# State-space scan and GELU feed-forward on one core: w_out loaded with four neighbouring rows to a partition, w_in cast with stepped writes, the last chunk stored from ScalarE

## The chip, the cores and the metric

The kernel runs on one core of a Trainium2 chip. The metric is the device time of one execution in microseconds (us); lower is better. Engines: PE is TensorE (PEld its weight loads), DVE is VectorE, ACT is ScalarE, POOL is GpSimd, SP is SyncE, which here only issues transfers. SPq and ACTq are the instructions with which SP and ACT issue transfers. A core has 16 DMA engines, which all queues share.

## The reference, cut to what matters

The first half is a chunked linear recurrence over four sequences of 768 tokens and 8 heads; its output, arranged as 3072 tokens by 256 features, goes into a feed-forward layer. Only the second half meets the change:

```python
n_tokens, d_model, d_ff = (3072, 256, 2048)
h = x @ w_in                       # (3072, 256) @ (256, 2048)
g = 0.5 * h * (1.0 + np.tanh(c * (h + 0.044715 * h * h * h)))
return (g @ w_out).astype(np.float32)   # (3072, 2048) @ (2048, 256)
```

The sum over the 2048 hidden features in the last product may be taken in any order, as long as column f of w_in meets row f of w_out.

## The kernel before, in words

The 3072 tokens are 24 chunks of 128 (`gc`, 0 to 23), taken in 12 pairs (`u`, 0 to 11). For each pair, the scan makes a masked gram matrix (`f_G` on PE, `f_M` on DVE), the outputs (`f_Y`), and a carried state (`f_S`, `f_SP`); its result is evicted as bf16 into `xm` with the features on the partitions (`f_yev`, L592). The feed-forward of the same pair follows: `f_s1` (L630) multiplies 128-column blocks of `w_in_sb` with the 256 tokens of the pair, two blocks to a PSUM bank; `f_gelu` (L645) evicts each bank through the GELU into `gT`, hidden features on the partitions; `f_s2` (L652) multiplies 16 blocks of `gT` with 16 slices of `w_out_sb` and sums them for one chunk; `f_oev` (L672) evicts the sum to `o_sb`, and `f_store` (L680) writes it out.

The weights come as float32 and are cast to bf16. Both are loaded in four quarters of 512 KB. `load_wi` (L208) brings 512 columns of w_in (rows of 2 KB) and is issued by ACT; `load_wo` (L280, the transfer at L283) brings 512 rows of w_out and is issued by SP. `wo` (L278) lays row `k*128 + f` on partition `f`, so each partition gets four separate rows of 1 KB. `f_wi` (L293) and `f_wo` (L296) cast a quarter each through `copy` (L285; POOL at L289, DVE at L291). POOL casts all quarters, but for the last of w_out, which it shares with DVE (`WENG`, L702).

The kernel writes its instructions in an order that a planner chooses at build time (`run_order`, L34): every step is a `Node` with an engine, a guessed duration, what it depends on and a priority, and each engine then executes its instructions in that fixed order. Loads are nodes as well: `LO` (L699) is the planner's guess, in us, for one quarter of w_out; `LI` that for w_in. `HEAD` (L700) is the order of the first loads: x 0, x 1, b 1, the three later quarters of w_in, b 2, w_out 0, w_out 1, c 2, w_out 2, w_out 3, x 2. Those in `SEND` go by ACT's queue, the rest by SP's. A load is issued only when the one eight before it has landed (`LANES`). The load of b 2 is also held by `f_gate` (L164), a one-element memset on POOL behind the first cast of w_in (L993, `GS = 0`), and the loads after it on SP stand behind it in the queue.

Chunks below `NPS` = 19 are stored by POOL, later ones by SP. The last chunk (L971 to L976) is evicted in two halves of 128 columns, one by ACT and one by DVE (`f_oevs`, L661), and each half is stored by a transfer of its own (`f_half`, L667), from ACT and from SP. Between planned gaps PE executes dummy products with zeros (`fill`, L1009) that keep it busy in the first 20 us of the plan.

Of the kernel before, what the change touches and what calls it, by code (L numbers as in the profile page):

```python
# [8 lines left out]
FP32 = mybir.dt.float32  # L9
# [104 lines left out]
def kernel(  # L114
# [10 lines left out]
    nc = tc.nc  # L125
# [3 lines left out]
    Q = 128  # L129
    CPB = S // Q  # L130
    NCH = batch * CPB
    T3 = CPB // 2
    W = S // T3
# [20 lines left out]
    opool = ctx.enter_context(tc.tile_pool(name="opool", bufs=6))  # L154
# [50 lines left out]
    WF = {}  # L205
# [58 lines left out]
    w_in_sb = const.tile([128, 2, d_ff], BF16, name="w_in_sb")  # L264
# [7 lines left out]

    X16 = {}
    state = {}
    gts, ops, hps, halves = {}, {}, {}, {}


    wo = moe_w_out.rearrange("(k f) m -> f k m", f=128)  # L278

    def load_wo(q, e):  # L280
        if ("o", q) not in WF:
            WF[("o", q)] = wfp.tile([128, 4, d_model], FP32, name="wf")
        e.dma_start(out=WF[("o", q)], in_=wo[:, 4 * q:4 * q + 4])  # L283

    def copy(eng, o, i):  # L285
        if eng == "ACT":
            nc.scalar.activation(o, i, AF.Copy)  # L287
        elif eng == "POOL":
            nc.gpsimd.tensor_copy(out=o, in_=i)  # L289
        else:  # L290
            nc.vector.tensor_copy(out=o, in_=i)  # L291

    def f_wi(q, k0, k1, eng):  # L293
        copy(eng, w_in_sb[:, k0:k1, q * 512:(q + 1) * 512], WF[("i", q)][:, k0:k1])

    def f_wo(q, k0, k1, eng):  # L296
        copy(eng, w_out_sb[:, 4 * q + 2 * k0:4 * q + 2 * k1], WF[("o", q)][:, 2 * k0:2 * k1])
# [360 lines left out]
                             rhs=w_out_sb[:, fi, :], start=(fi == 0), stop=(fi == NF - 1),  # L658
                             skip_group_check=True)

    def f_oevs(gc, h, eng):  # L661
        hs = slice(h * 128, h * 128 + 128)
        o_sb = opool.tile([128, 128], FP32, name="o_half")
        copy(eng, o_sb, ops[gc][:, hs])
        halves[h] = o_sb

    def f_half(gc, h, q):  # L667
        u, r = divmod(gc, 2)
        hs = slice(h * 128, h * 128 + 128)
        q.dma_start(out=out[u * W + r * Q:u * W + (r + 1) * Q, hs], in_=halves[h])  # L670

    def f_oev(gc, eng):  # L672
        o_sb = opool.tile([128, d_model], FP32, name="o_sb")
        if eng == "ACT":
# [19 lines left out]
    DW = 1.0  # L694
    LANES = 8
    FIRST = [("c", 3), ("b", 3), ("c", 4), ("x", 3), ("b", 4), ("x", 4)]
    NPS = 19
    PET = {0: "ACT", 1: "ACT", 2: "ACT", 3: "ACT"}
    LB, LX, LI, LO, XD, XL = 0.92, 1.25, 1.42, 1.5, 0.6, 3.6  # L699
    HEAD = [("x", 0), ("x", 1), ("b", 1), ("wi", 1), ("wi", 2), ("wi", 3), ("b", 2), ("wo", 0), ("wo", 1), ("c", 2), ("wo", 2), ("wo", 3), ("x", 2)]  # L700
    SEND = {("b", 1): -185, ("wi", 1): -184.9, ("wi", 2): -179.5, ("wi", 3): -179.4}
    WENG = [("POOL", "POOL", "POOL", "POOL"), ("POOL", "POOL", "POOL", "POOL+DVE")]  # L702
# [1 line left out]
    TAIL = 4  # L704
# [3 lines left out]
    GS = 0  # L708
# [15 lines left out]
    def add(eng, dur, fn, *args, deps=(), prio=0.0, alloc=(), done=0.0):  # L724
        n = Node(eng, dur, (lambda: fn(*args, *[BK[j] for p, j in zip(n.alloc, n.bank)
                                               if p == "bk"])), deps, prio, alloc, done)
        nodes.append(n)
        return n
# [5 lines left out]
    def frees(n, *by, i=0):  # L734
        if n.alloc:
            n.frees[i] += list(by)
# [12 lines left out]
    win_l, won_l, wi_n, wo_n = {}, {}, {}, {}  # L749
    bl, xl, xcn = {}, {}, {}  # L750
    later = []
    Gn, Mn, Yn, yevn, Sn, SPn, Fn, bnn, gcn, Dns = ({} for _ in range(10))
# [77 lines left out]
    for j in range(NP):  # L830
# [58 lines left out]
        u = j  # L889
# [63 lines left out]
    for g, (c0, n) in enumerate(GROUPS):  # L953
        per = 512 // (n * Q)
        ends_ = []
        for tt in range(n):
            gc = c0 + tt
            if g < TWO and tt:
                prev = ahead
            ahead = list(prev)  # L960
            for q in range(4):
                need = [geln[(g, i)] for i in range(4 * n) if i * per <= 4 * q + 3]
                nd = add("PE", 0.437, f_s2, g, tt, q, deps=need[-1:] + wo_n[q] + prev,
                         prio=PB + 10 * c0 + 10 * n + 2.5 * ((tt + 2 * q) if g < TWO else 4 * tt + q) + 1.2,
                         alloc="bk" if q == 0 else ())
                if q == 0:
                    first = nd
                prev = [nd]
            ends_.append(nd)
            oeng = "DVE" if gc >= NCH - TAIL and gc % 2 else "ACT"  # L970
            if gc == NCH - 1:  # L971
                ev2 = [add(e, 0.25, f_oevs, gc, h, e, deps=[nd], prio=-40 + h) for h, e in enumerate(("ACT", "DVE"))]
                frees(first, *ev2)
                s0 = add("ACT", 0.1, f_half, gc, 0, nc.scalar, deps=[ev2[0]], prio=-39)
                add("OUT", 0.05, f_half, gc, 1, nc.sync, deps=[ev2[1], s0], prio=gc)
                continue  # L976
            else:
                oevn[gc] = add(oeng, 0.4, f_oev, gc, oeng, deps=[nd], prio=-40)
            frees(first, oevn[gc])
            if g < TWO:  # L980
                prev = list(ends_)
            if gc < NPS:
                st_n = add("POOL", 1.1, f_store, gc, nc.gpsimd, deps=[oevn[gc]], prio=2000)
            else:
                add("OUT", 0.05, f_store, gc, nc.sync, deps=[oevn[gc]], prio=gc)

    if D1 is not None:
        Dns[1].deps.append(gpn[(0, D1)])
# [1 line left out]
        n.deps.append(gpn[(u, 0)])  # L990

    held = HEAD[max(n for n, e in enumerate(HEAD) if e in SEND) + 1]
    issue[held].deps.append(add("POOL", 0.1, f_gate, *held, deps=[SPn[0] if GS else wi_n[0][-1]], prio=-98))  # L993
    for g in range(GT_BUFS, len(GROUPS)):
        c0, n = GROUPS[g - GT_BUFS]
        gpn[(g, 0)].deps.append(oevn[c0 + n - 1])
# [54 lines left out]
```

## Time and profile before

| | |
|---|---|
| median of 2 runs | 115.31 us (115.06 to 115.55) |
| the profiled execution's own time | 115.72 us |
| its span in the trace | 114.0 us |
| PE busy | 106.8 us (94%) |
| ACT, DVE, POOL busy | 73.1, 59.0, 32.2 us |
| moved by DMA | 15.01 MB in 68,736 packets |
| granted clock of PE | 1.00 throughout |

In a row of a timeline stand the start and the length in us, the engine, the line, the operation, what it writes and reads, and how many instructions are merged; in brackets stands how long the engine was idle before, and what ended the wait. A row of windows has a stretch, its length, the busy time and the number of instructions of PE, PEld, DVE, ACT and POOL, the granted clock, the mean busy share of the 16 DMA engines (transfers that overlap in one engine can bring it over 1) and GB/s. A queue row has the packets, the MB, and the time of its packets as a share of 16 engines' span.

### The profile page before, as it was taken

What the parts mean: (1) busy time and instruction counts of PE and PEld (TensorE: products, weight loads), DVE (VectorE), ACT (ScalarE), POOL (GpSimd) and SP (SyncE); (2) the same over time, 40 slices, a digit from 0 to 9 for tenths busy, and PEclk for the clock granted to TensorE, in tenths of its full rate; (3) what the DMA queues carried; (4) which work ended last, traced back from release to release, by engine and by line L of the source; (5) the groups of instructions that cost most, each with busy time, mean ns of one, the idle gap of its engine ahead of it and who ended that gap; (6) DMA issues with size and microseconds to landing.
All of it is one profiled execution on the core that took longest, in us unless ns stands there. A gap on an engine that the chain in (4) does not pass through costs nothing.

```text
span 114.0 us, 3606 instructions
## 1 busy us (share of the span) xinstructions
PE 106.8 (94%) x1497; PEld 86.5 (76%) x1497; DVE 59.0 (52%) x134; ACT 73.1 (64%) x161; POOL 32.2 (28%) x60
## 2 busy tenths in 40 slices
PE   5968998979999999999999999999999999999990
PEld 2544566958688788887887887888878878878870
DVE  2799764287796193750962944906918318000101
ACT  0557796951559368596685794774966866857720
POOL 6851636657510412103241311312211011000000
PEclk9999999999999999999999999999999999999999
DMA  3999976959977959599898877776121111011021
GB/s 69 264 311 384 354 200 207 286 98 231 181 137 146 121 109 154 82 161 117 138 125 162 131 85 152 107 102 129 46 46 46 52 45 50 6 46 46 0 92 46
DMA packets 68736, 15.01 MB, mean 132 GB/s; under 512 B 64176, under 2 KB 67088, under 8 KB 68720
## 3 DMA queue, kind: packets, MB, share of 16 engines
q1 hardware_dynamic: 63456, 9.74, 49.5%
q10 hardware_dynamic: 4352, 2.56, 7.2%
q0 software_dynamic: 912, 2.49, 5.9%
q8 instruction: 11, 0.18, 0.6%
q14 instruction: 5, 0.04, 0.1%
HBM read 10.58 MB, written 3.15 MB: 120 GB/s over the span
## 4 chain that ended last, share of the span: by engine, by line
PE 76%; DMA 11%; SPq 5%; POOL 3%; issue 2%; ACTq 1%; DVE 0%; ACT 0%; POOLq 0%
PE bk L657 37%; PE bk L640 31%; DMA wf<-in_moe_w_out_dram 7%; DMA wf<-in_moe_w_in_dram 5%; SPq L283 3%; PE bk L524 2%; POOL w_out_sb L289 2%; PE gb L454 2%; SPq L183 1%; PE bk L498 1%; ACTq L183 1%; POOL w_in_sb L289 1%; PE bk L547 1%; PE gb L465 1%; PE bk L510 0%
## 5 line engine op out<-in xcount | busy, mean ns | idle before, releaser
L648 ACT ACTIVATE gT<-bk 128x512 bf16<-128x512 f32 x96 | 50.4, 603 | 9.1 <-PE bk L640 8.9
L657 PE MATMUL bk<-w_out_sb,gT 128*128 128x256 bf16 x384 | 49.1, 273 | 0.6 <-POOL w_out_sb L289 0.6
L640 PE MATMUL bk<-xm,w_in_sb 128*128 128x256 bf16 x384 | 47.5, 273 | 0.8 <-POOL w_in_sb L289 0.8
L640 PEld LDWEIGHTS <-w_in_sb 128*128 128x128 bf16 x384 | 37.0, 98 | 6.1 <-POOL w_in_sb L289 1.5
L657 PEld LDWEIGHTS <-gT 128*128 128x128 bf16 x384 | 36.5, 98 | 6.7 <-issue 2.4
L683 POOL DMA_DIRECT2D out_dram<-o_sb x19 | 10.5, 553 | 45.4 <-ACT o_sb L675 45.4
L475 DVE TENSOR_TENSOR m<-gb,trk 128x1024 bf16<-128x1024 f32 x14 | 17.0, 1217 | 0.0
L675 ACT ACTIVATE o_sb<-bk 128x256 f32<-128x256 f32 x22 | 8.5, 386 | 11.3 <-PE bk L657 5.2
L607 DVE SCALAR_TENSOR_TENSOR s_new<-s_new,pend,bk 128x64 f32<-128x64 f32 x16 | 4.4, 276 | 20.4 <-ACT xm L287 19.7
L287 ACT ACTIVATE xm<-bk 128x256 bf16<-128x256 f32 x22 | 7.4, 381 | 9.2 <-PE bk L498 6.9
L384 DVE TENSOR_TENSOR bc<-bc,fac 128x256 bf16<-128x256 f32 x24 | 10.9, 481 | 3.0 <-DMA bc<-in_C_dram 2.0
L289 POOL CAST x<-x_t 128x512 bf16<-128x512 f32 x12 | 8.3, 690 | 10.6 <-DMA x_t<-in_x_dram 10.6
L475 DVE TENSOR_TENSOR m<-gb,tri 128x1024 bf16<-128x1024 f32 x8 | 9.7, 1219 | 1.5 <-PE gb L465 1.5
L623 DVE SCALAR_TENSOR_TENSOR sp_new<-s_new,pend,pm 128x128 bf16<-128x128 f32 x19 | 7.4, 420 | 0.1
L1013 PE MATMUL gb<-wz 128*128 128x512 bf16 (+2 forms) x17 | 5.4, 444 | 1.3 <-DVE warm L221 1.3
L430 DVE TENSOR_SCALAR ce<-bt,par 128x256 bf16<-128x256 bf16 x22 | 5.3, 284 | 2.2 <-ACT bt L287 2.2
L677 DVE COPY o_sb<-bk 128x256 f32<-128x256 f32 x1 | 0.4, 425 | 10.9 <-PE bk L657 10.9
L1013 PEld LDWEIGHTS <-wz 128*128 128x128 bf16 x25 | 2.7, 120 | 3.8 <-issue 1.9
L289 POOL CAST w_in_sb<-wf 128x1024 bf16<-128x1024 f32 x4 | 4.2, 1040 | 3.3 <-DMA wf<-in_moe_w_in_dram 3.3
L605 DVE COPY s_new<-bk 128x64 f32<-128x64 f32 x3 | 0.7, 222 | 8.1 <-ACT xm L287 8.1
L289 POOL CAST w_out_sb<-wf 128x1024 bf16<-128x1024 f32 (+1 forms) x4 | 4.0, 995 | 3.1 <-DMA wf<-in_moe_w_out_dram 3.1
L287 ACT ACTIVATE bt<-bk 128x256 bf16<-128x256 bf16 (+1 forms) x5 | 2.4, 473 | 1.7 <-PE bk L406 1.7
(81 smaller groups left out, 58.2 us busy)
## 6 DMA issues: line engine op xcount, KB each, us to landing
out_dram<-o_sb POOLq DMA_DIRECT2D x19, 128.0 KB, 2.9
wf<-in_moe_w_in_dram ACTq DMA_DIRECT2D x4, 512.0 KB, 8.3
wf<-in_moe_w_out_dram SPq DMA_DIRECT2D x4, 512.0 KB, 8.3
x_t<-in_x_dram SPq DMA_DIRECT2D x14, 128.0 KB, 3.0
x_t<-in_x_dram SPq DMA_DIRECT2D x5, 256.0 KB, 4.5
bc<-in_C_dram SPq DMA_DIRECT2D x14, 64.0 KB, 3.5
bc<-in_B_dram SPq DMA_DIRECT2D x14, 64.0 KB, 3.4
bc<-in_C_dram SPq DMA_DIRECT2D x4, 128.0 KB, 4.6
```

The costliest lines, as they stand in the source:

```text
L287: nc.scalar.activation(o, i, AF.Copy)
L289: nc.gpsimd.tensor_copy(out=o, in_=i)
L384: nc.vector.tensor_tensor(out=d["bc16"][:, i], in0=d["bc"][:, i].rearrange("p h (r n) -> p r h n", r=2) if j < TOK else d["bc"][:, i].rear ...
L430: nc.vector.tensor_scalar(out=d["ce"][:, e], in0=v, scalar1=par[:, e:e + 1], scalar2=None, op0=ALU.mult)
L475: nc.vector.tensor_tensor(out=state[("m", u, f)].rearrange("p g r e t -> p g (r e t)"), in0=state.pop(("gc", u, f), gram[f]).rearrange("p ...
L623: nc.vector.scalar_tensor_tensor(out=sp_new.rearrange("p (j d) -> p j d", j=2), in0=state[("s", gc)].rearrange("p (o d) -> p o d", o=1).to ...
L640: nc.tensor.matmul(out=hp[:, j * nt:(j + 1) * nt], lhsT=w_in_sb[:, kc, fi * 128:(fi + 1) * 128], rhs=xm[:, kc, c0 * Q:c0 * Q + nt], start= ...
L648: nc.scalar.activation(gts[g][:, i * per:(i + 1) * per, 0:nt], hps.pop((g, i)).rearrange("p (j t) -> p j t", j=per), AF.Gelu_apprx_tanh)
L657: nc.tensor.matmul(out=ops[gc], lhsT=gts[g][:, fi, tt * Q:(tt + 1) * Q], rhs=w_out_sb[:, fi, :], start=(fi == 0), stop=(fi == NF - 1), ski ...
L675: nc.scalar.activation(o_sb, ops.pop(gc), AF.Copy)
L683: q.dma_start(out=o.rearrange("(p r) m -> r p m", r=2)[r] if u < TOK else o[r * Q:(r + 1) * Q], in_=ops.pop(gc))
L1013: nc.tensor.matmul(out=bank[:, 0:128 * w], lhsT=wz[:, 0:128], rhs=wz[:, 0:128 * w], start=True, stop=True)
```

## The change

`wo` now takes the 2048 rows as four quarters of 128 groups of four: partition `f` of quarter `q` gets rows `512q + 4f` to `512q + 4f + 3`, which are 4 KB in a row in memory. Slice `4q + k` of `w_out_sb` then holds rows `512q + 4f + k`, so the columns of w_in have to be put in the same order: `f_wi` reads its quarter in a row and writes neighbouring elements 128 elements (256 bytes) apart, so that block `4q + k` of `w_in_sb` holds columns `512q + 4f + k`. The casts of w_out and all products keep their shapes.

Chunk 18 is stored by SP in place of POOL (`NPS` 18). The last chunk is evicted whole by ACT and stored by one transfer that ACT issues; `f_oevs` and `f_half` go. The planner's guess for a quarter of w_out goes from 1.5 to 1.3 us. The list at `f_gate` gets more entries, of which `GS = 0` still picks the first, the same as before.

```diff
-    wo = moe_w_out.rearrange("(k f) m -> f k m", f=128)
+    wo = moe_w_out.rearrange("(q f k) m -> q f k m", q=4, k=4)
...
-        e.dma_start(out=WF[("o", q)], in_=wo[:, 4 * q:4 * q + 4])
+        e.dma_start(out=WF[("o", q)], in_=wo[q])
...
     def f_wi(q, k0, k1, eng):
-        copy(eng, w_in_sb[:, k0:k1, q * 512:(q + 1) * 512], WF[("i", q)][:, k0:k1])
+        copy(eng, w_in_sb[:, k0:k1, q * 512:(q + 1) * 512].rearrange("d c (k f) -> d c f k", k=4),
+             WF[("i", q)][:, k0:k1].rearrange("d c (f k) -> d c f k", k=4))
...
-    def f_oevs(gc, h, eng):
...
-    def f_half(gc, h, q):
...
-    NPS = 19
+    NPS = 18
...
-    LB, LX, LI, LO, XD, XL = 0.92, 1.25, 1.42, 1.5, 0.6, 3.6
+    LB, LX, LI, LO, XD, XL = 0.92, 1.25, 1.42, 1.3, 0.6, 3.6
...
-            oeng = "DVE" if gc >= NCH - TAIL and gc % 2 else "ACT"
-            if gc == NCH - 1:
-                ev2 = [add(e, 0.25, f_oevs, gc, h, e, deps=[nd], prio=-40 + h) for h, e in enumerate(("ACT", "DVE"))]
-                frees(first, *ev2)
-                s0 = add("ACT", 0.1, f_half, gc, 0, nc.scalar, deps=[ev2[0]], prio=-39)
-                add("OUT", 0.05, f_half, gc, 1, nc.sync, deps=[ev2[1], s0], prio=gc)
-                continue
-            else:
-                oevn[gc] = add(oeng, 0.4, f_oev, gc, oeng, deps=[nd], prio=-40)
+            oeng = "DVE" if gc >= NCH - TAIL and gc % 2 and gc < NCH - 1 else "ACT"
+            oevn[gc] = add(oeng, 0.4, f_oev, gc, oeng, deps=[nd], prio=-40)
             frees(first, oevn[gc])
...
-                add("OUT", 0.05, f_store, gc, nc.sync, deps=[oevn[gc]], prio=gc)
+                last = gc == NCH - 1
+                add("ACT" if last else "OUT", 0.05, f_store, gc, nc.scalar if last else nc.sync, deps=[oevn[gc]], prio=gc)
...
-    issue[held].deps.append(add("POOL", 0.1, f_gate, *held, deps=[SPn[0] if GS else wi_n[0][-1]], prio=-98))
+    issue[held].deps.append(add("POOL", 0.1, f_gate, *held, deps=[(wi_n[0][-1], SPn[0], xcn[1], SPn[1])[GS]], prio=-98))
```

More of the change, by code (lines that the diff above doesn't have):

```diff
@@ L274 @@
     state = {}
-    gts, ops, hps, halves = {}, {}, {}, {}
-    wo = moe_w_out.rearrange("(k f) m -> f k m", f=128)
+    gts, ops, hps = {}, {}, {}
+    wo = moe_w_out.rearrange("(q f k) m -> q f k m", q=4, k=4)
     def load_wo(q, e):
@@ L659, in f_s2 @@
                              skip_group_check=True)
-    def f_oevs(gc, h, eng):
[L662 to L665, printed above, removed]
-    def f_half(gc, h, q):
-        u, r = divmod(gc, 2)
-        hs = slice(h * 128, h * 128 + 128)
-        q.dma_start(out=out[u * W + r * Q:u * W + (r + 1) * Q, hs], in_=halves[h])
     def f_oev(gc, eng):
```

## The prediction

> **What bounds the kernel now.** I read the page first: the engines, the chain that ended last, then PE in time.
>
> ```profile
> span 114.0 us, 3606 instructions
> PE 106.8 (94%) x1497; PEld 86.5 (76%) x1497; DVE 59.0 (52%) x134; ACT 73.1 (64%) x161; POOL 32.2 (28%) x60
> ...
> PE 76%; DMA 11%; SPq 5%; POOL 3%; issue 2%; ACTq 1%; DVE 0%; ACT 0%; POOLq 0%
> ```
>
> PE is busy for 94% of the span, and 76% of the chain is PE. So no edit away from PE can be worth more than the time in which PE waits. A window says where that is not:
>
> ```profile
> 50.00:110.00 60.00, 60.00 (x791) 51.37 (x790) 25.16 (x53) 41.62 (x90) 10.45 (x17) 1.00 0.46 82
> ```
>
> From 50 to 110 us PE is busy for all of 60.00 us at granted clock 1.00, and its timeline has no idle note between 24.80 us and that window either. What the change can gain lies before 24.80 us or behind the last product. PE's timeline of the start:
>
> ```profile
> 14.79 1.05 PE L640 MATMUL bk<-xm,w_in_sb 128*128 128x256 bf16 x8 [0.28 <-POOL w_in_sb L289]
> 15.67 0.33 PE L1013 MATMUL bk<-wz 128*128 128x256 bf16 x2
> 15.93 0.25 PE L535 MATMUL bk<-bt,sp_new 64*32 64x128 bf16 x8
> ...
> 17.75 2.36 PE L640 MATMUL bk<-xm,w_in_sb 128*128 128x256 bf16 x20 [0.49 <-POOL w_in_sb L289]
> ...
> 23.76 0.42 PE L465 MATMUL gb<-ce,bt 32*64 32x256 bf16 x16
> 24.80 2.78 PE L657 MATMUL bk<-w_out_sb,gT 128*128 128x256 bf16 x24 [0.62 <-POOL w_out_sb L289]
> ```
>
> Three waits in a row: 0.28 us for the third cast of w_in, 0.49 us for the fourth, and 0.62 us for the last cast of w_out. Between 17.75 and 24.18 us PE is dense, and at 24.18 it stands: its order has nothing else until the last quarter of w_out is there. So PE resumes at the later of two times: the end of its own work, now 24.18, and the last cast of w_out, now 24.80.
>
> POOL, which makes these casts (the x casts are here for their lengths):
>
> ```profile
> 7.35 1.04 POOL L289 CAST w_in_sb<-wf 128x1024 bf16<-128x1024 f32 x1 [0.43 <-DMA wf<-in_moe_w_in_dram]
> ...
> 12.36 1.04 POOL L289 CAST w_in_sb<-wf 128x1024 bf16<-128x1024 f32 x1 [0.64 <-DMA wf<-in_moe_w_in_dram]
> 13.70 1.04 POOL L289 CAST w_in_sb<-wf 128x1024 bf16<-128x1024 f32 x1 [0.29 <-DMA wf<-in_moe_w_in_dram]
> 16.66 1.04 POOL L289 CAST w_in_sb<-wf 128x1024 bf16<-128x1024 f32 x1 [1.93 <-DMA wf<-in_moe_w_in_dram]
> 18.34 1.04 POOL L289 CAST w_out_sb<-wf 128x1024 bf16<-128x1024 f32 x1 [0.65 <-DMA wf<-in_moe_w_out_dram]
> 19.69 1.04 POOL L289 CAST w_out_sb<-wf 128x1024 bf16<-128x1024 f32 x1 [0.31 <-DMA wf<-in_moe_w_out_dram]
> 21.62 1.04 POOL L289 CAST w_out_sb<-wf 128x1024 bf16<-128x1024 f32 x1 [0.89 <-DMA wf<-in_moe_w_out_dram]
> 23.88 0.87 POOL L289 CAST w_out_sb<-wf 128x512 bf16<-128x512 f32 x1 [1.23 <-DMA wf<-in_moe_w_out_dram]
> ...
> 30.70 0.62 POOL L289 CAST x<-x_t 128x512 bf16<-128x512 f32 x1
> ...
> 39.13 0.62 POOL L289 CAST x<-x_t 128x512 bf16<-128x512 f32 x1
> ```
>
> Each cast of a weight begins when its transfer lands; POOL was idle before every one. The landings of w_out, not POOL, set 24.80. And these landings are slowed by one lagging DMA engine:
>
> ```profile
> 16.50:17.00 0.50, 0.50 (x8) 0.43 (x6) 0.01 (x1) 0.38 (x2) 0.34 (x1) 1.00 0.07 23
> 17.00:17.50 0.50, 0.26 (x3) 0.09 (x1) 0.50 (x1) 0.28 (x3) 0.50 (x1) 1.00 0.07 25
> ```
>
> A DMA share of 0.07 is about one engine of 16 (0.0625), although two quarters of w_out have not landed yet: 15 engines have finished and a transfer counts as landed when the last one has. SP stands meanwhile in an issue:
>
> ```profile
> 8.86 1.61 SPq L283 DMA_DIRECT2D wf<-in_moe_w_out_dram  x1
> 10.52 2.14 SPq L283 DMA_DIRECT2D wf<-in_moe_w_out_dram  x1
> 12.70 1.32 SPq L183 DMA_DIRECT2D bc<-in_C_dram  x1
> 14.06 2.98 SPq L283 DMA_DIRECT2D wf<-in_moe_w_out_dram  x1
> ```
>
> **The change: w_out with rows of 4 KB.** A quarter goes from 512 packets of 1 KB to 128 of 4 KB, so from 32 to 8 on each engine. The price of a packet comes from the queue rows:
>
> ```profile
> q1 hardware_dynamic: 63456, 9.74, 49.5%
> q10 hardware_dynamic: 4352, 2.56, 7.2%
> q0 software_dynamic: 912, 2.49, 5.9%
> ```
>
> The shares times 16 x 114 us are 903, 131 and 108 us. With a ns for each packet and b us for each MB, q1 and q0 give a = 8.0 and b = 40.3; q10 then comes out at 35 + 103 = 138 us against 131, so the split holds to 5%. A quarter has 24 packets fewer on an engine: 24 x 8.0 = 0.19 us, and four quarters 0.77 us at the lagging engine, where they are served one behind the other (the casts at 18.34 and 19.69 stand 1.35 us apart, 32 packets by 42 ns). The last quarter then lands near 23.1 us, its cast ends near 24.0, and PE resumes at 24.18: a gain of 0.62 us, not 0.77. The lower end is 0, if the lagging engine is paced by bytes or by something else. There is more at the upper end (the issue of 2.98 us is waiting for room in the queue, by its length against the 1.32 beside it, so later loads move up too), but 24.18 caps it: none of it counts.
>
> The Trainium skill ("DMA: Bandwidth & Descriptors", section "Why small descriptors are slow (HBM only)") puts the cost of a packet in the DMA engine at about 3 cycles; at the 850 MHz which that page gives for the fabric that is an estimate of 3.5 ns, not 8.0. By it the sum would gain only some 0.34 us here in place of 0.62, and the time would be 0.3 us longer; the queue rows of this trace bear out the larger price.
>
> What is late next once this wait is gone: 24.18 itself, so the casts of w_in. After that nothing, as far as rows show; the scan's later steps on DVE are fed by PE and move along with it.
>
> **w_in cast with stepped writes.** Four instructions, same elements, each written 256 bytes from the last. No row of this trace has a POOL instruction that writes single elements in steps, so I bound the extra time x of one cast. The nearest rows are the x casts: the one at 30.70 (pair 4) reads in jumps after every 32 elements, that at 39.13 (pair 5) reads in a row, and both take 0.62 us. From 512 to 1024 elements the cast grows by 0.42 us, so 0.82 ns for an element and 0.2 us fixed. If POOL spends its time on elements, x = 0; that is also the lower end, since nothing gets shorter. The upper end I set at three times the time for an element, x = 1.7 us. I take 0, by the x casts, which are the nearest rows, though they show jumps between runs and not single elements; this is the weakest step.
>
> Where x lands: the first cast (7.35) also releases the memset that holds the load of b 2 on SP; b 2, w_out 0 and 1 and the rest of SP's queue stand behind it. An x of some 0.5 there is covered, as the lagging engine, not the issue, sets when these land. The delay of the second and third cast reaches PE at 14.79; 0.27 us of dummy products, then 0.49 us of waiting before 17.75 cover up to some 0.76. The fourth starts on its landing at 16.66, and PE behind it at 17.75 moves by all of x. PE's own work then ends at 24.18 + x, against a w_out cast at 24.0: x up to 0.62 eats the gain, more is a loss.
>
> **The last chunk and the stores.** The end of the kernel, PE first and then ACT, DVE and SP:
>
> ```profile
> 106.80 4.09 PE L657 MATMUL bk<-w_out_sb,gT 128*128 128x256 bf16 x36
> ...
> 109.23 0.38 ACT L675 ACTIVATE o_sb<-bk 128x256 f32<-128x256 f32 x1 [1.58 <-issue]
> 110.93 0.28 ACT L287 ACTIVATE o_half<-bk 128x128 f32<-128x128 f32 x1 [1.31 <-PE bk L657]
> 111.24 0.29 DVE L291 COPY o_half<-bk 128x128 f32<-128x128 f32 x1 [3.38 <-ACT o_half L287]
> 111.56 0.33 SPq L670 DMA_DIRECT2D out_dram<-o_half  x1
> ```
>
> ```profile
> out_dram<-o_sb SPq DMA_DIRECT2D x4, 128.0 KB, 1.7
> ...
> out_dram<-o_half SPq DMA_DIRECT2D x1, 64.0 KB, 1.6
> ```
>
> The halves don't run side by side: DVE's starts when ACT's has ended, so the last issue comes at 111.56. Afterwards one eviction of 0.38 us, then the issue by ACT near 110.93 + 0.38 + 0.03 = 111.34: 0.22 us earlier. The transfer is twice as large and lands in 1.7 and not 1.6 us, so the gain is 0.1 us (from 0 to 0.2). Nothing is queued behind it on ACT. Chunk 18 goes from POOL to SP: one of POOL's 19 issues (553 ns) is saved, one of about 0.33 us comes on SP. I cost it at nothing, as SP issues nothing between 84.27 and 100.29 us, and what stands behind are stores of later chunks only; without that cover it would cost its 0.33 us:
>
> ```profile
> L683 POOL DMA_DIRECT2D out_dram<-o_sb x19 | 10.5, 553 | 45.4 <-ACT o_sb L675 45.4
> ```
>
> ```profile
> 83.05 1.22 SPq L395 DMA_TRANSPOSE bt<-bc  x1
> 100.29 9.69 SPq L683 DMA_DIRECT2D out_dram<-o_sb  x4
> ```
>
> **The planner's 1.3.** The four landings are planned up to 0.8 us earlier, so PE's order may put products with w_out ahead of one or two groups of four w_in products (0.44 us each). If the real landings are earlier by 0.77 us, this costs nothing; if they are not, PE waits up to 0.44 us longer. I take 0.
>
> The sum on the profiled execution: 115.72 - 0.62 - 0.10 + 0 = 115.0 us. The median of the runs shown, 115.31, is 0.41 us below that execution, so 114.6 us.
>
> **The rivals.** (1) Stepped writes cost about half as much again for an element. Then x = 0.4 to 0.6, PE's own work ends near 24.75 and the gain is spent: about 115.1 us. Against it speaks that jumps in the x casts cost nothing; for it, that those jumps come every 32 elements. In a sentence of its own: the Trainium skill ("SBUF — State Buffer", section "Door 1: The DMA port swizzle (why `[64,N]` ≈ `[32,N]`)") says that accesses run at full rate only with at least two hits in the same line of 16 bytes, which a step of 256 bytes never has. No run so far shows whether that holds for POOL's writes.
>
> (2) The transfers don't come earlier: the lagging engine is paced by its bytes, or lags by as much again. PE's wait of 0.62 us stays, and only the end gains: 115.2 us. For it: the landings of the third and fourth quarter stand 1.93 and 2.26 us behind the one before, more than the 1.35 us for 32 packets. Against it: the packet price from the queue rows.
>
> (3) The other side: stepped writes cost more than twice as much. POOL then makes three casts of w_in back to back from 12.36: they end at 12.36 + 3 x (1.04 + x) + 0.1, past the fourth landing's 17.70 + x once x is over 1.05. With x = 1.3 (casts of 2.34 us) PE starts at 19.5 in place of 17.75, ends its own work near 25.9, and the time is 115.31 + 1.1 - 0.1 = 116.3. It decides from x = 0.72, where the sum is zero; over 2% it takes x near 1.7.
>
> **How the numbers follow.** The forecast has 0.45, rival 1 has 0.28, rival 2 has 0.15, rival 3 has 0.12. The range reaches over rivals 1 and 2 and into 3: from 114.1 (the forecast with 0.2 at the end and the spread of the runs, 0.25 to either side) to 116.1. The likeliest case's own range is 114.2 to 115.0. A measurement of this kernel can tell about 2%, or 2.3 us, from no change. Faster by that needs 1.4 us and more than all the waits that the change reaches: 0.02. Slower needs the upper end of rival 3: 0.07. Within: 0.91.
>
> **What would show each step.** In the profile of the changed kernel: 61,920 packets in q1 (63,456 less 1,536), and the issues of w_out short; casts of w_in at 1.04 us (rival 1: 1.4 to 1.6, rival 3: over 2); the last cast of w_out ending near 24.0 us and no idle note ahead of the products with its quarter; PE's last product some 0.6 us earlier; the last issue on ACT 0.41 us behind PE's end. It would be wrong if a new wait of PE shows behind 24 us, or if the casts are longer.

## The result, and the profile after

The changed kernel takes 130.31 us (130.31 to 130.32, 2 runs) against 115.31 before: a ratio of 1.1325 (95% interval 1.1272 to 1.1379), 15.0 us slower. The prediction said 114.6 us, 114.1 to 116.1. The profiled execution took 130.31 us with a span of 128.6, the one before 115.72 and 114.0: 14.6 us to account for. Here and below a median is of all runs, while a ratio leaves out the runs that fell in a slower state of the chip.

The page of the changed kernel, for the rows that the prediction showed of before: span, engines, chain, queues, and the group of the casts. In a group's row stand the busy time and the mean length in ns, then the idle time ahead of them.

```profile
span 128.6 us, 3602 instructions
...
PE 109.5 (85%) x1496; PEld 87.8 (68%) x1497; DVE 73.7 (57%) x133; ACT 73.6 (57%) x161; POOL 45.6 (35%) x59
...
PEclk9995586557999999999999999999999999999999
...
q1 hardware_dynamic: 61920, 9.80, 46.8%
...
PE 81%; DVE 13%; issue 4%; ACT 0%; ACTq 0%; DVEq 0%
...
L289 POOL CAST w_in_sb<-wf 128x1024 bf16<-128x1024 f32 x4 | 19.0, 4947 | 0.7 <-DMA wf<-in_moe_w_in_dram 0.7
```

Read it against the prediction's rows. POOL is busy 13.4 us longer; four instructions alone add 14.8, casts of 4.95 us in place of 1.04. DVE is busy 14.7 us longer with one instruction fewer, and has entered the chain with 13%, although the change gives DVE no new work and takes the eviction of a half from it. The transfers are what was meant: 61,920 packets. The clock row lies between 5 and 8 tenths from the fourth to the tenth slice.

POOL's timeline of the changed kernel:

```profile
7.29 4.73 POOL L289 CAST w_in_sb<-wf 128x1024 bf16<-128x1024 f32 x1 [0.49 <-DMA wf<-in_moe_w_in_dram]
...
12.75 14.24 POOL L289 CAST w_in_sb<-wf 128x1024 bf16<-128x1024 f32 x3 [0.22 <-DMA wf<-in_moe_w_in_dram]
26.58 3.84 POOL L289 CAST w_out_sb<-wf 128x1024 bf16<-128x1024 f32 x4
```

Three casts now run back to back and the last ends at 12.75 + 14.24 = 26.99, where it ended at 16.66 + 1.04 = 17.70. The casts of w_out find their data there and run in 3.84 us.

DVE's timeline of the same time, and behind it the row of the first of these steps in the kernel before:

```profile
7.44 5.17 DVE L359 CAST pm<-par 128x128 bf16<-128x128 f32 x1
...
13.46 1.23 DVE L476 TENSOR_TENSOR m<-gb,tri 128x1024 bf16<-128x1024 f32 x1 [0.35 <-PE gb L466]
14.60 3.03 DVE L476 TENSOR_TENSOR m<-gs,tri 128x1024 bf16<-128x1024 bf16 x1
17.55 4.85 DVE L431 TENSOR_SCALAR ce<-bt,par 128x256 bf16<-128x256 bf16 x2
22.32 4.32 DVE L385 TENSOR_TENSOR bc<-bc,fac 128x256 bf16<-128x256 f32 x1
26.57 0.41 DVE L291 CAST xm<-bk 128x256 bf16<-128x256 f32 x1
```

```profile
6.89 0.23 DVE L358 CAST pm<-par 128x128 bf16<-128x128 f32 x1
```

The cast of `pm` takes 5.17 us where it took 0.23; the two instructions for `ce` take 4.85 in place of 0.47, `bc` 4.32 in place of 0.41. They end at 12.61, 17.63 (`m` from `gs`), 22.40 and 26.64, and those are about the times at which one POOL cast ends and the next begins (the third begins at 17.30, the fourth at 21.85 and ends at 26.99). What is not held reads a PSUM bank: `m<-gb,tri` keeps its 1.23 us and the cast of `xm` from a bank its 0.41. A copy from a bank, `bt`, that starts at 11.39, before `pm` has ended, also takes 1.22 us in place of 0.28; it ends together with `pm`, at 12.61.

PE's timeline of the changed kernel:

```profile
18.09 0.39 PE L997 MATMUL gb<-wz 128*128 128x512 bf16 x1
26.70 0.39 PE L407 MATMUL bk<-ident,bc 128*128 128x128 bf16 x2 [8.21 <-DVE bc L385]
...
27.37 1.04 PE L641 MATMUL bk<-xm,w_in_sb 128*128 128x256 bf16 x4
28.33 0.65 PE L466 MATMUL gb<-ce,bt 32*64 32x256 bf16 x16
28.92 3.08 PE L641 MATMUL bk<-xm,w_in_sb 128*128 128x256 bf16 x20
...
33.25 2.35 PE L641 MATMUL bk<-xm,w_in_sb 128*128 128x256 bf16 x20
```

PE stands for 8.21 us, and not for POOL: it waits for DVE's `bc`. Only at 27.37 does it begin the products that it began at 11.96 before, and the 20 products behind the fourth cast, at 17.75 before, begin at 33.25: 15.5 us later. Behind that it runs as before. It gets 0.9 us back by its end (125.47 against 110.89, so 14.6), 0.62 of it the wait at 24.80, which isn't there as w_out was cast long ago.

One window of each kernel, before first, says what the stage lost (PE, PEld, DVE, ACT, POOL):

```profile
7.00:27.00 20.00, 17.40 (x283) 12.84 (x282) 14.02 (x29) 14.70 (x35) 10.95 (x14) 1.00 0.91 255
```

```profile
7.00:27.00 20.00, 5.31 (x87) 2.55 (x88) 19.54 (x14) 3.63 (x12) 19.49 (x7) 0.66 0.99 270
...
28.00:30.00 2.00, 2.00 (x24) 0.97 (x23) 1.13 (x2) 1.51 (x2) 2.00 (x3) 0.50 0.86 80
```

In the same 20 us PE does 87 matmuls in place of 283, DVE 14 instructions in place of 29 while it counts as busy for 19.54 us. Busy is not work here. When PE resumes, it does so at granted clock 0.50: four products take 1.04 us, where the same four took 0.61 before.

The end of the changed kernel, ACT and its queue:

```profile
125.56 0.38 ACT L665 ACTIVATE o_sb<-bk 128x256 f32<-128x256 f32 x1 [1.36 <-PE bk L658]
125.97 0.37 ACTq L673 DMA_DIRECT2D out_dram<-o_sb  x1
```

The store is issued 0.41 us behind the start of the eviction, as in the prediction's sum (0.38 + 0.03; behind PE's end it is 0.50, where the prediction's list of signs has 0.41 and its own figures make 0.45), and the span ends 3.0 us behind that start (128.6 - 125.56), against 3.1 before (114.0 - 110.93).

### The profile page after: what moved, and what is told of

Read it like the earlier page. It is cut to its first block, busy times and chain, and to the rows that moved or that the text cites. A ratio compares the mean times of both kernels' runs of the same rounds, so it can differ in the third digit from the quotient of the medians.

```text
span 128.6 us, 3602 instructions
## 1 busy us (share of the span) xinstructions
PE 109.5 (85%) x1496; PEld 87.8 (68%) x1497; DVE 73.7 (57%) x133; ACT 73.6 (57%) x161; POOL 45.6 (35%) x59
## 3 DMA queue, kind: packets, MB, share of 16 engines
q1 hardware_dynamic: 61920, 9.80, 46.8%
q0 software_dynamic: 864, 2.36, 4.8%
## 4 chain that ended last, share of the span: by engine, by line
PE 81%; DVE 13%; issue 4%; ACT 0%; ACTq 0%; DVEq 0%
PE bk L658 34%; PE bk L641 34%; DVE bc L385 4%; DVE ce L431 4%; DVE m L476 3%; PE gb L997 3%; PE bk L525 2%; PE gb L466 2%; PE gb L455 1%; PE bk L499 1%; DVE bt L291 1%; PE bk L548 1%; PE gb L311 1%; PE bk L407 1%; PE bk L575 1%
## 5 line engine op out<-in xcount | busy, mean ns | idle before, releaser
L641 PE MATMUL bk<-xm,w_in_sb 128*128 128x256 bf16 x384 | 48.3, 277 | 0.0
L641 PEld LDWEIGHTS <-w_in_sb 128*128 128x128 bf16 x384 | 37.9, 99 | 5.2 <-issue 0.4
L289 POOL CAST w_in_sb<-wf 128x1024 bf16<-128x1024 f32 x4 | 19.0, 4947 | 0.7 <-DMA wf<-in_moe_w_in_dram 0.7
L385 DVE TENSOR_TENSOR bc<-bc,fac 128x256 bf16<-128x256 f32 x24 | 13.8, 610 | 0.1
L431 DVE TENSOR_SCALAR ce<-bt,par 128x256 bf16<-128x256 bf16 x22 | 9.7, 510 | 4.5 <-ACT bt L287 4.5
L407 PE MATMUL bk<-ident,bc 128*128 128x128 bf16 x16 | 2.2, 245 | 8.4 <-DVE bc L385 8.4
L624 DVE SCALAR_TENSOR_TENSOR sp_new<-s_new,pend,pm 128x128 bf16<-128x128 f32 x19 | 8.6, 483 | 0.1
L407 PEld LDWEIGHTS <-bc 128*128 128x128 bf16 x16 | 1.3, 108 | 9.4 <-DVE bc L385 9.3
L997 PE MATMUL gb<-wz 128*128 128x512 bf16 (+2 forms) x17 | 6.1, 488 | 1.3 <-DVE warm L221 1.3
L466 PE MATMUL gb<-ce,bt 32*64 32x256 bf16 x80 | 2.6, 333 | 4.9 <-DVE fac L330 4.9
```

The source lines that it names most:

```text
L385: nc.vector.tensor_tensor(out=d["bc16"][:, i], in0=d["bc"][:, i].rearrange("p h (r n) -> p r h n", r=2) if j < TOK else d["bc"][:, i].rear ...
L431: nc.vector.tensor_scalar(out=d["ce"][:, e], in0=v, scalar1=par[:, e:e + 1], scalar2=None, op0=ALU.mult)
L624: nc.vector.scalar_tensor_tensor(out=sp_new.rearrange("p (j d) -> p j d", j=2), in0=state[("s", gc)].rearrange("p (o d) -> p o d", o=1).to ...
L641: nc.tensor.matmul(out=hp[:, j * nt:(j + 1) * nt], lhsT=w_in_sb[:, kc, fi * 128:(fi + 1) * 128], rhs=xm[:, kc, c0 * Q:c0 * Q + nt], start= ...
L997: nc.tensor.matmul(out=bank[:, 0:128 * w], lhsT=wz[:, 0:128], rhs=wz[:, 0:128 * w], start=True, stop=True)
```

## The experiments

What had to be told apart: whether the cast alone does all this; what in it costs (the step, the short runs, the lines touched); and which of two effects makes 15 us, the weights being late or DVE being held. Times stand against runs of the kernel before on the same chip (its medians there were 115.31 to 115.57).

**The cast alone.** The kernel before with the changed `f_wi` and nothing else; the columns of w_in then meet other rows of w_out.

```diff
-        copy(eng, w_in_sb[:, k0:k1, q * 512:(q + 1) * 512], WF[("i", q)][:, k0:k1])
+        copy(eng, w_in_sb[:, k0:k1, q * 512:(q + 1) * 512].rearrange("d c (k f) -> d c f k", k=4),
+             WF[("i", q)][:, k0:k1].rearrange("d c (f k) -> d c f k", k=4))
```

> The kernel before with the stepped write of w_in alone; w_out, the stores and the planner's figure stay, so columns of w_in meet the wrong rows of w_out. Theory W (the stepped casts are the whole loss): 130 to 131.5 us, since the 0.7 us that the other parts were to gain is missing. Rival M (another part of the change costs as well): under 128 us.

Measured: 131.17 us (129.97 to 131.38, 4 runs), ratio 1.1323 (1.1256 to 1.1391). The stepped cast alone makes the whole loss.

**Forms of the cast.** The kernel before, with casts appended behind the last store: 1024 elements as before, as after (steps on the write), and with the steps on the read; then smaller ones with one size varied, on POOL alone. `tsrc` and `tdf` are float32, `tdst` is bf16.

```diff
+    def forms(e):
+        copy(e, tdst[:, 0:1024], tsrc)
+        copy(e, tdst[:, 0:1024].rearrange("d (c k f) -> d c f k", c=2, k=4),
+             tsrc.rearrange("d (c f k) -> d c f k", c=2, k=4))
+        copy(e, tdst[:, 0:1024].rearrange("d (c k f) -> d c k f", c=2, k=4),
+             tsrc.rearrange("d (c f k) -> d c k f", c=2, k=4))
...
+        for n, s in ((512, 1), (512, 2), (512, 4), (512, 8), (512, 12), (128, 32)):
+            copy(e, tdst[:, 0:n * s].rearrange("d (n s) -> d n s", s=s)[:, :, 0], tsrc[:, 0:n])
...
+        for n, s in ((512, 2), (256, 4), (256, 1)):
+            copy(e, tdf[:, 0:n * s].rearrange("d (n s) -> d n s", s=s)[:, :, 0], tsrc[:, 0:n])
...
+    forms("POOL")
...
+    forms("DVE")
+    forms("ACT")
```

> The kernel before, with casts of a weight tile appended behind its last store, on POOL first, then DVE, then ACT: 128x1024 in a row, with the change's stepped write, and with a stepped read and a write in a row; on POOL also 512 elements in one long run with write steps of 1, 2, 4, 8 and 12 elements, 128 elements with a step of 32, runs of 4 with gaps of 4, and float32 outputs. Its total time is not compared. Theory W (each write that leaves its neighbourhood costs): the change's form takes 4.5 to 5.0 us on POOL, the long stepped ones grow from 0.62 to about 2.3 us at some step, runs of 4 stay near 0.7, the stepped read stays near 1.0 to 1.5. Rival S (the short innermost count of 4 costs, not the step): the long stepped ones all stay near 0.62 us and the runs of 4 take over 2 us. On DVE and ACT both expect under 2 us for the change's form.

The first three casts of each engine in its timeline, in the order row, stepped write, stepped read:

```profile
112.62 1.04 POOL L289 CAST xm<-wf 128x1024 bf16<-128x1024 f32 x1 [17.67 <-ACT wf L1026]
113.72 4.73 POOL L289 CAST xm<-wf 128x1024 bf16<-128x1024 f32 x1
118.51 1.98 POOL L289 CAST xm<-wf 128x1024 bf16<-128x1024 f32 x1
```

```profile
132.00 0.69 DVE L291 CAST xm<-wf 128x1024 bf16<-128x1024 f32 x1
132.73 2.73 DVE L291 CAST xm<-wf 128x1024 bf16<-128x1024 f32 x1
135.50 1.07 DVE L291 CAST xm<-wf 128x1024 bf16<-128x1024 f32 x1
```

```profile
136.68 1.06 ACT L287 ACTIVATE xm<-wf 128x1024 bf16<-128x1024 f32 x1 [24.13 <-DVE xm L291]
137.77 4.75 ACT L287 ACTIVATE xm<-wf 128x1024 bf16<-128x1024 f32 x1
142.55 2.00 ACT L287 ACTIVATE xm<-wf 128x1024 bf16<-128x1024 f32 x1
```

4.73 us on POOL and 4.75 on ACT: the price isn't POOL's own, and my expectation for DVE and ACT missed. Steps on the read, 16 bytes, cost 0.94 us, steps on the write 3.69. With 512 elements of bf16 written every 2, 4, 8, 16 and 24 bytes POOL took 0.61, 0.75, 1.32, 2.45 and 2.42 us: it grows with the step up to 16 bytes and no further. Runs of four with gaps of four took 0.61. So the price is one of lone elements. Lone elements of float32 cost as well, but less; POOL's rows for 256 of them written every 16 bytes, and for 256 in a row:

```profile
130.47 0.63 POOL L289 COPY wf<-wf 128x256 f32<-128x256 f32 x1
131.17 0.40 POOL L289 COPY wf<-wf 128x256 f32<-128x256 f32 x1
```

**Pairs and singles.** The same method, with 512 elements, to separate two readings: that each new line of memory (16 bytes) costs, or that each write smaller than a word does. An aligned pair of bf16 is a word of 4 bytes.

```diff
+        for s in (4, 8):
+            copy(e, tdst[:, 0:512 * s].rearrange("d (n s) -> d n s", s=s)[:, :, 0], tsrc[:, 0:512])
+        for r, s in ((2, 8), (2, 16), (4, 16)):
+            copy(e, tdst[:, 0:512 // r * s].rearrange("d (n s) -> d n s", s=s)[:, :, 0:r],
+                 tsrc[:, 0:512].rearrange("d (n r) -> d n r", r=r))
+        copy(e, tdst[:, 0:2048].rearrange("d (n s) -> d n s", s=8)[:, :, 1:3],
+             tsrc[:, 0:512].rearrange("d (n r) -> d n r", r=2))
+        copy(e, tdf[:, 0:1024].rearrange("d (n s) -> d n s", s=8)[:, :, 0], tsrc[:, 0:128])
```

> The kernel before with casts of 512 elements appended behind its last store, on POOL, DVE and ACT in turn: in a row, single bf16 elements 8 and 16 bytes apart, pairs 16 and 32 bytes apart, runs of four 32 bytes apart, pairs that start at an odd element, and 128 single float32 elements 32 bytes apart; its total time is not compared. Theory H (a write of less than 4 bytes to a place of its own is what costs, whatever the line): pairs take half of a single's price per element or less, near 0.65 us, odd pairs 2.4 us or more. Rival N (every new line of 16 bytes costs 4.4 ns): pairs take 1.3 us at 16 bytes and at 32 bytes alike, even or odd, and the float32 singles 0.76 us, where theory H gives them 0.3 to 0.45.

POOL's timeline; after the cast in a row come singles every 8 and every 16 bytes, aligned pairs every 16 and every 32 bytes, runs of four every 32 bytes, and pairs that start at an odd element, every 16 bytes:

```profile
112.41 0.61 POOL L289 CAST xm<-wf 128x512 bf16<-128x512 f32 x1 [16.88 <-ACT wf L1026]
113.08 1.32 POOL L289 CAST xm<-wf 128x512 bf16<-128x512 f32 x1
114.47 2.45 POOL L289 CAST xm<-wf 128x512 bf16<-128x512 f32 x1
116.98 0.63 POOL L289 CAST xm<-wf 128x512 bf16<-128x512 f32 x1
117.68 0.65 POOL L289 CAST xm<-wf 128x512 bf16<-128x512 f32 x1
118.38 0.61 POOL L289 CAST xm<-wf 128x512 bf16<-128x512 f32 x1
119.06 1.32 POOL L289 CAST xm<-wf 128x512 bf16<-128x512 f32 x1
```

An aligned pair in a line of its own takes no longer than two elements in a row (0.63 and 0.65 against 0.61); a single there costs 2.45. DVE and ACT say the same: 0.43 us in a row, 1.30 for singles every 16 bytes and 0.43 for pairs on DVE, 0.63, 2.46 and 0.66 on ACT. So it is not the new line that makes 4.4 ns, but the write of half a word in it. A new line isn't free either: the lone float32, a whole word each, took 0.63 us for 256 and, in this run, 0.42 for 128 written every 32 bytes; (0.63 - 0.2) / 256 and (0.42 - 0.2) / 128 both make 1.7 ns for a line. Two elements in a row take 1.64 ns, so a pair in a line shows nothing of it.

The odd pairs took 1.32 and not the 2.4 or more that I expected. One count gives all of POOL's figures for half words: 0.2 us, and 4.4 ns for each visit to a line of 16 bytes in which half a word is written, however many halves that visit writes. Singles every 4, 8 and 16 bytes and the odd pairs visit 128, 256, 512 and 256 lines, which makes 0.76, 1.33, 2.45 and 1.33 us; measured were 0.75, 1.32, 2.45 and 1.32. Steps of 24 bytes visit 512 lines again and took 2.42. In the changed kernel's cast neighbours are written 256 bytes apart, so each of its 1024 elements is a visit. The count was made from these figures; no further run tests it.

**Four casts in a row.** To part lateness from the hold on DVE: POOL is kept as long, by ordinary casts. The kernel before casts each quarter of w_in four times over, 4 x 1.04 us being close to one stepped cast.

```diff
-        copy(eng, w_in_sb[:, k0:k1, q * 512:(q + 1) * 512], WF[("i", q)][:, k0:k1])
+        for _ in range(4):
+            copy(eng, w_in_sb[:, k0:k1, q * 512:(q + 1) * 512], WF[("i", q)][:, k0:k1])
```

> As the five casts in a row, with four: by the 1.13 us that one of the repeated casts took there, POOL ends its casts of w_in near 27 us, where the one stepped cast ends them (26.99), so POOL is equally late and only the holding differs. Theory L (one long cast also holds DVE until it ends, and that adds some 6 us): PE starts the fourth quarter within 0.1 us of the last cast, near 27 us, and the time is 124.5 us (123.5 to 126). Rival P (only POOL's lateness counts): 129.5 to 131.5.

Measured: 124.6 us, median of 4 (123.48 to 125.64), before 115.5 there. The profiled execution took 123.85. Its POOL, then its PE:

```profile
12.67 13.50 POOL L289 CAST w_in_sb<-wf 128x1024 bf16<-128x1024 f32 x12
```

```profile
21.75 1.89 PE L641 MATMUL bk<-xm,w_in_sb 128*128 128x256 bf16 x8 [3.16 <-POOL w_in_sb L289]
...
26.23 2.36 PE L641 MATMUL bk<-xm,w_in_sb 128*128 128x256 bf16 x20 [0.73 <-POOL w_in_sb L289]
```

POOL is through at 26.17, 0.8 us before the changed kernel. But PE has done the third group meanwhile and goes on 0.06 us behind POOL, at 26.23 and not at 33.25. No row of DVE between 7 and 18 us is longer than 1.65 us here: a step that meets a short cast waits for that one cast, not for the 4.7 us. So the weights' lateness makes 123.85 - 115.5 = 8.4 us. The profiled execution of the cast alone took 130.98, 7.1 more; POOL's casts end 1.0 us later there (27.20 against 26.17), and the other 6.1 us come with the long hold of DVE. The two ran on different chips, but the kernel before took 115.57 and 115.5 us there.

**Five casts in a row.** The same, once more over.

```diff
-        for _ in range(4):
+        for _ in range(5):
```

> The kernel before, in which each cast of w_in is made five times over, in a row, so POOL is busy for the same 5 us with a quarter, but in pieces of 1 us; nothing else changes. Theory L (lateness of POOL's casts makes some 9 us, and the rest comes since one long cast holds DVE's own casts, products and scalings until it ends): about 124 us, 122 to 126, DVE steps at most about 1 us longer than before. Rival P (only POOL's lateness counts, whether it holds DVE or not): 129.5 to 131.5 as with the stepped write alone.

Measured: 129.51 us (128.11 to 129.74, 4 runs), ratio 1.1178 (1.1098 to 1.1258). The 124 that pure lateness was to give missed, but because the casts took 1.13 us each and POOL ended with w_in at 30.76, 3.8 us behind the changed kernel's; PE's fourth group began right behind, at 30.82. By itself the time looked like that of the long hold; the place in the timeline, and the run with four, told otherwise.

**The change with the cast in a row.** Everything else of the change kept; again the columns meet other rows.

```diff
-        copy(eng, w_in_sb[:, k0:k1, q * 512:(q + 1) * 512].rearrange("d c (k f) -> d c f k", k=4),
-             WF[("i", q)][:, k0:k1].rearrange("d c (f k) -> d c f k", k=4))
+        copy(eng, w_in_sb[:, k0:k1, q * 512:(q + 1) * 512], WF[("i", q)][:, k0:k1])
```

> The changed kernel with the cast of w_in in a row, so that columns of w_in meet the wrong rows of w_out; everything else as changed. Theory W: this is the prediction's sum with x = 0, 114.6 us (114.2 to 115.0), the last cast of w_out ends before PE needs it, and PE's wait of 0.62 us is gone. Rival M: over 116 us. A third way, the prediction's rival 2: 115.2, with the wait still there.

Measured: 115.43 us, median of 12, ratio 0.9966 (0.9929 to 1.0003): about 0.4 us where the prediction's terms made 0.7, and an interval that just includes no change. In its profile the last cast of w_out ends at 21.92 and PE doesn't wait for it; but its own work ends at 25.37 and not 24.18, with a new wait of 0.53 us for DVE's `xm`.

**The end alone.** Of the change, only the last chunk's eviction and store and `NPS` 18; w_out, w_in and the planner's 1.5 as before; the edit is shown against the changed kernel.

```diff
-    wo = moe_w_out.rearrange("(q f k) m -> q f k m", q=4, k=4)
+    wo = moe_w_out.rearrange("(k f) m -> f k m", f=128)
...
-        copy(eng, w_in_sb[:, k0:k1, q * 512:(q + 1) * 512].rearrange("d c (k f) -> d c f k", k=4),
-             WF[("i", q)][:, k0:k1].rearrange("d c (f k) -> d c f k", k=4))
+        copy(eng, w_in_sb[:, k0:k1, q * 512:(q + 1) * 512], WF[("i", q)][:, k0:k1])
...
-    LB, LX, LI, LO, XD, XL = 0.92, 1.25, 1.42, 1.3, 0.6, 3.6
+    LB, LX, LI, LO, XD, XL = 0.92, 1.25, 1.42, 1.5, 0.6, 3.6
```

> The changed kernel with w_out's rows, w_in's cast and the planner's 1.5 us put back: only the last chunk by ACT and chunk 18 by SP remain of the change. The prediction's term: 0.1 us (0 to 0.2) below the kernel before. Rival: the end costs or gains 0.3 us or more.

Measured: 115.02 us, median of 12, ratio 0.9974 (0.9944 to 1.0005): 0.3 us, with 0.1 and zero inside the interval. It told something else. Its w_out is that of before, in packets of 1 KB; POOL, then PE:

```profile
21.47 0.61 POOL L289 CAST w_out_sb<-wf 128x512 bf16<-128x512 f32 x1 [0.31 <-DMA wf<-in_moe_w_out_dram]
```

```profile
24.15 0.42 PE L465 MATMUL gb<-ce,bt 32*64 32x256 bf16 x16
24.51 2.68 PE L657 MATMUL bk<-w_out_sb,gT 128*128 128x256 bf16 x23
```

The last quarter is cast at 22.08, and no idle note stands ahead of the products with it. The run with the appended forms, whose head is that of before too, shows the same (cast at 22.91, products at 23.93 without a wait), and so does the run with pairs and singles (21.46 and 24.52). So PE's wait of 0.62 us at 24.80 was one of the profiled execution, and not one that the kernel always has: with the same transfers POOL's last cast of w_out ended anywhere from 21.46 to 24.75.

**Steps on the read.** The change, but with the cast reading every fourth element (16 bytes) and writing in a row.

```diff
-        copy(eng, w_in_sb[:, k0:k1, q * 512:(q + 1) * 512].rearrange("d c (k f) -> d c f k", k=4),
-             WF[("i", q)][:, k0:k1].rearrange("d c (f k) -> d c f k", k=4))
+        copy(eng, w_in_sb[:, k0:k1, q * 512:(q + 1) * 512].rearrange("d c (k f) -> d c k f", k=4),
+             WF[("i", q)][:, k0:k1].rearrange("d c (f k) -> d c k f", k=4))
```

> The changed kernel with the cast of w_in turned round: it reads every fourth column (a step of 16 bytes) and writes in a row; the product is the reference's. The appended forms gave 1.98 us for it, so x = 0.94. Theory W, with the prediction's rule for x (PE's own work ends at 24.18 + x, the last w_out cast earlier): 115.31 + 0.94 - 0.62 - 0.1 = 115.5, and no more than 116.5 with DVE held by POOL a little longer. Rival: the layout itself costs, or POOL's longer casts hold DVE so often that it stays above 118 us.

Measured: 117.85 us, median of 6, ratio 1.0167 (1.0104 to 1.0229); over the 116.5 at most that I gave it. Its profiled execution took 120.39 us, so I take only lengths from it: the casts took 2.04 us in the mean, and DVE was held again (the cast of `pm` 1.94 us). A cast of 2 us is already enough to cost; how much of it is lateness and how much comes through DVE isn't parted here.

**Steps in the weight load.** The cast in a row, and PE picks every fourth column when it loads weights, a step of 8 bytes:

```diff
-                                 lhsT=w_in_sb[:, kc, fi * 128:(fi + 1) * 128],
+                                 lhsT=w_in_sb[:, kc, fi // 4 * 512:(fi // 4 + 1) * 512]
+                                 .rearrange("d (f k) -> d k f", k=4)[:, fi % 4],
```

> The changed kernel with the cast of w_in in a row, and the new order of the columns taken by TensorE instead: the weight load of a block reads every fourth column (a step of 8 bytes). The product is the reference's. If a stepped weight load takes the 98 ns of one in a row, the same time as e3_row_cast to 0.3 us; if it takes twice that, it is longer than the 109 ns between products and the 384 loads add 30 us or more.

Measured: 121.34 us, ratio 1.0495 (1.0443 to 1.0547), between what the theories gave. The groups of the casts say why:

```profile
L289 POOL CAST w_in_sb<-wf 128x1024 bf16<-128x1024 f32 x4 | 4.2, 1040 | 5.9 <-PE bk L640 4.7 <-DMA wf<-in_moe_w_in_dram 1.2
```

POOL waits 4.7 us for PE before it casts the next quarter, although that quarter's columns are read by nobody yet. All four share one tile, so I took the waits to be dependencies that the build made too wide for a stepped read, and tried a tile for each quarter.

**Two neighbouring rows.** w_out with two rows to a run, packets of 2 KB; the cast reads every second element, 8 bytes, and writes in a row. Everything else is the change.

```diff
-    wo = moe_w_out.rearrange("(q f k) m -> q f k m", q=4, k=4)
+    wo = moe_w_out.rearrange("(q h f k) m -> q f h k m", q=4, h=2, k=2)
...
+        copy(eng, w_in_sb[:, k0:k1, q * 512:(q + 1) * 512].rearrange("d c (h k f) -> d c h k f", h=2, k=2),
+             WF[("i", q)][:, k0:k1].rearrange("d c (h f k) -> d c h k f", h=2, k=2))
```

> The changed kernel with two neighbouring rows of w_out to a partition (256 packets of 2 KB for a quarter), and a cast of w_in that reads every second column (a step of 8 bytes) and writes in a row; the product is the reference's. Theory W: two float32 elements lie in each 16 bytes that are read, so the cast stays near 1.04 us; the transfers keep two thirds of the gain: 114.9 us (114.5 to 115.4), 0.3 to 0.8 below the kernel before on the same chip. Rival: any step in the cast costs, 1.3 us or more each, and the time is that of the kernel before or longer.

Measured: 114.99 us, median of 12, ratio 0.9956 (0.9912 to 1.0000). The casts took 1.10 us at the least: steps of 8 bytes on the read cost 0.06. The same kernel again, on another chip:

> The same kernel as e8_two_rows, on whatever chip comes, to see whether its 0.4% over the kernel before holds: 0.9956 again (0.991 to 1.000) if it is the kernel, 1.000 if it was chance.

114.97 us, median of 12, ratio 0.9959 (0.9926 to 0.9993).

**Steps in the weight load, a tile for each quarter.**

```diff
-    w_in_sb = const.tile([128, 2, d_ff], BF16, name="w_in_sb")
+    w_in_sb = [const.tile([128, 2, 512], BF16, name=f"w_in_sb{q}") for q in range(4)]
...
+        copy(eng, w_in_sb[q][:, k0:k1], WF[("i", q)][:, k0:k1])
...
+                                 lhsT=w_in_sb[fi // 4][:, kc].rearrange("d (f k) -> d k f", k=4)[:, fi % 4],
```

> The stepped weight loads of e5_lhs_steps, with a tile of its own for each quarter of the bf16 w_in; the product is the reference's. Theory D (the 6 us that e5_lhs_steps lost come from POOL's casts waiting for TensorE's loads of other quarters in the same tile, not from the 113 ns of a stepped load): 115.0 us, within 0.3 us of e3_row_cast's place, 0.3 to 0.8 below the kernel before on the same chip. Rival: the longer loads cost by themselves, 384 x 4 ns or more where they pass the 109 ns between products: 117 us or more.

Measured: 114.7 us, median of 12, before 115.44; ratio 0.9939 (0.9902 to 0.9977). It has the lowest ratio of all versions, 0.7 us under the kernel before, though its interval overlaps those of the end alone, the cast in a row and two neighbouring rows. Its groups:

```profile
L289 POOL CAST w_in_sb<-wf 128x1024 bf16<-128x1024 f32 x4 | 4.5, 1132 | 1.8 <-DMA wf<-in_moe_w_in_dram 1.8
...
L640 PEld LDWEIGHTS <-w_in_sb 128*128 128x128 bf16 x384 | 41.9, 113 | 0.8 <-issue 0.4
```

POOL waits for its transfers alone, so the 4.7 us came with the shared tile. A weight load with steps takes 113 ns in place of 98, and PE's products don't show it: 20 of them take 2.35 us at 18.34, as in the kernel before at 17.75 (2.36).

## Why the prediction was wrong

**The failed step: x = 0.** The prediction took the extra time of a stepped cast as nothing, "by the x casts, which are the nearest rows", and set the upper end at 1.7 us. It is 3.7 us (4.73 in place of 1.04), and over four casts 3.9 in the mean. An element costs 4.4 ns, (4.73 - 0.2) / 1024, against 0.82: more than five times, where the upper end was three. The x casts could not show it, since they read in jumps after every 32 elements and write in a row; what costs is a write of a lone bf16. No row of before had one. A bound that rests on a factor of my choosing isn't a bound by rows: with no row near, the upper end should have stayed open, or the sign left to the rivals. The range didn't even reach that bound: by rival 3's own rule x = 1.7 makes 117.5 us, and the range ended at 116.1.

The Trainium skill's rule that stood beside rival 1 ("SBUF — State Buffer", section "Door 1: The DMA port swizzle (why `[64,N]` ≈ `[32,N]`)") pointed the right way. With whole words the traces agree with it: 256 lone float32 took 0.63 us against 0.40 in a row, 512 written every 8 bytes, two to a line, took no longer than those 256 (0.63), and aligned pairs, two elements to a line of 16 bytes, ran at full rate (0.63 against 0.61 us). With half words they differ from it: odd pairs have two elements to a line as well and took 1.32 us, singles every 4 bytes have four and took 0.75.

**The rule for what x does: "24.18 + x".** It followed one cast. Above 1.05 us the casts are serial on POOL, as rival 3 said, and its formula 12.36 + 3 x (1.04 + x) + 0.1 with x = 3.7 gives 26.7, where POOL ended at 26.99. So the rival's mechanism was right and its size was not; lateness by itself is 8.4 us of the 15 (four casts in a row).

What no rival had is DVE. The prediction said that "the scan's later steps on DVE are fed by PE and move along with it"; in the changed kernel PE waits 8.21 us for one of these steps. The prediction listed who waits for POOL's output and not who shares memory with POOL while it runs. The Trainium skill ("SBUF — State Buffer", section "Who interferes with whom") says that a GpSimd instruction which reads SBUF and a DVE instruction with two inputs in SBUF, or one in a mode that uses both of DVE's ports, exclude each other, and that the later one waits for the whole of the earlier. This case's rows agree: 5.17 us for a cast of 0.23, and no hold on `m<-gb,tri`, which reads one input from PSUM (1.23 us); in which mode the cast ran, no row shows. In the kernel before, DVE's `bc` shows the same beside POOL's casts of 1.04 us (1.05 at 7.61, 0.41 at 10.71 with POOL idle), and a step loses about one cast at most; at 4.7 us the hold put DVE behind POOL for 12 us in a row, and PE behind DVE, so that products with the early quarters of w_in, which had been cast long before, came only when the fourth cast was through: 6 us more. Some 1.0 us of these is the clock. The rows of PE in before that answer to those at 27.37, 28.33 and 28.92 (with the 8 at 14.79):

```profile
11.96 0.61 PE L640 MATMUL bk<-xm,w_in_sb 128*128 128x256 bf16 x4
12.50 0.42 PE L465 MATMUL gb<-ce,bt 32*64 32x256 bf16 x16
12.86 1.65 PE L640 MATMUL bk<-xm,w_in_sb 128*128 128x256 bf16 x12
```

There 0.61 + 0.42 + 1.65 + 1.05 = 3.73 us, in the changed kernel 1.04 + 0.65 + 3.08 = 4.77.

**w_out in packets of 4 KB.** Packet count right. The gain of 0.62 us was wrong: its wait belonged to one execution, as three others with the old transfers show. With the cast in a row the last w_out cast ends at 21.92; in the kernel with the end alone, at 22.08. I can't tell a gain of this part from none.

**The last chunk.** Right in place (issue 0.41 us behind the eviction's start) and within what can be measured in size: 0.1 predicted, 0.3 measured with an interval from -0.1 to 0.6. For **chunk 18 and the planner's 1.3**, costed at nothing, no row shows a cost, and no run has them alone.

**The rest of the change** is worth 0.4 us with the cast in a row (interval 0 to 0.8) and 0.5, 0.5 and 0.7 us with two neighbouring rows (twice) and with the steps in the weight load, so the direction holds once the steps are moved (the last two intervals end below no change, at 0.9993 and 0.9977). How it divides between w_out and the end stays open: the versions' intervals overlap with that of the end alone.

## What to carry to other kernels

Keep writes of bf16 in aligned pairs or longer runs; if an order has to change, put the step on a read of up to 8 bytes (0.06 us for a cast of 1.04 here) or into PE's weight load, with a tile of its own for each part that is written separately. Before lengthening a POOL instruction, list DVE's steps that work from SBUF to SBUF and run beside it: four of them were held here until a cast of POOL ended, and PE behind them. And before pricing a wait, look for it in a second execution.

## What the runs showed of the hardware

Singles of bf16 written every 4, 8 and 16 bytes cost POOL 0.75, 1.32 and 2.45 us for 512, ACT the same within 0.02 where it ran them (1.34, 2.46), DVE about half (0.73, 1.30). By the differences, a visit to a line of 16 bytes that writes half a word takes 4.4 ns on POOL and ACT and 2.2 on DVE ((2.46 - 1.34) / 256, (1.30 - 0.73) / 256). Aligned pairs cost no more than elements in a row on any of the three. Lone float32 cost POOL 1.7 ns each: 0.63 us for 256 every 16 bytes, 0.42 for 128 every 32.

After 8 us without work PE's products took 1.04 us for four in place of 0.61, at granted clock 0.50 until 30 us; from 31 us on it was 1.00. The trace of the cast alone has the same 1.04 us at the same place while its clock row shows 1.00 throughout: there the lengths of the products are the surer sign.
